# Chunk-selected attention with a gated feed-forward layer: mask halves by block transposes, x scaled on either of two engines, loads planned with a margin, first block's turns leading

## The chip, the cores and the metric

The kernel runs on one core of a Trainium2 chip. A core has a matrix engine (TensorE, PE in the profile; its weight loads are PEld) and three engines for everything else: VectorE (DVE), ScalarE (ACT) and GpSimd (POOL). SyncE (SP) issues transfers. Each engine takes its instructions strictly in program order and waits at an instruction until its inputs are there. The metric is the device time of the whole program in microseconds (us).

## The reference

```python
# q, k, v: (4, 8, 768, 64); chunks of 32 keys, the 6 best chunks for each query
k_min, k_max = k_chunks.min(3), k_chunks.max(3)
ub = sum_d max(q * k_min, q * k_max)              # upper bound of the score of each chunk
ub = where(causal, ub, -1e9); top = argsort(ub)[..., -6:]
scores = where(chunk in top and key <= query, q @ k.T / 8, -1e9)
attn = softmax(scores) @ v                        # -> x: (3072, 512)
xn = x / sqrt(mean(x * x) + 1e-6) * rms_g
g, val = xn @ w_gate, xn @ w_val                  # 512 -> 1536
out = (g * sigmoid(g) * val) @ w_out              # 1536 -> 512
```

## The kernel before

The work is cut into 12 blocks of 256 tokens (4 batches by 3). Each block goes through an attention part (two jobs of four heads) and a feed-forward part (`ffn`). A small planner in the kernel's Python (`Plan`) holds all operations with a guessed length, a priority and their inputs, and simulates the engines: the order that comes out of the simulation is the program. It does not run on the chip. An operation made with `flex` can go to any of several engines; the planner picks one. A lower priority number comes first among what is ready at the same time.

```python
PACE, LEAD = 23.0, 60.0
def due_attn(i): return PACE * i - LEAD      # priority of block i's attention
def due_ffn(i):  return PACE * i             # and of its feed-forward part
SPLIT = {0}                                  # the first block: its two halves of tokens apart
...                                          # (cut) in Rings: when a planned transfer lands
op.done = now + (0.9 if op.dma[2] else 1.2)
...                                          # (cut) in job(i, g): one block, four heads
turn("k"); half("k")                         # VectorE: kT by 32x32 block transposes; then kb in bf16
                                             # (ScalarE or GpSimd)
... # ext: minimum and maximum per chunk (VectorE); dk, bd: placed in BD (GpSimd or VectorE)
turn("q"); half("q")                         # qT, qb
... # upper: bounds (TensorE); ubn, bar, top, mk (VectorE): mk = bound below the sixth best
plan.op("mt", "DVE", ... VE.transpose(out=mtd, in_=mk) ...)     # the mask, transposed in 32x32 blocks

def swap():                                  # the mask's two halves of 64 partitions exchanged
    VE.tensor_copy(at(mto)[0:64, 0:nj], at(mtd)[64:128, 0, 0:nj])
    VE.tensor_copy(at(mto)[64:128, 0:nj], at(mtd)[0:64, 1, 0:nj])
def swap_act(): ...                          # the same two copies as ScalarE activations
flex("swap", {"DVE": (0.46, 0.48, swap), "ACT": (0.65, 0.66, swap_act)}, base + 3,
     reads=[mtd], writes=[mto], ...)
... # vx: v in bf16 with a column of ones (GpSimd or ScalarE)
... # scores: q k (L643) plus the mask as matmuls of mtd and mto (L654); exp (ScalarE) -> pt;
    # tri: the causal triangle of pt (GpSimd); values: pt v (L719); rden, norm -> xnat (VectorE)

def norm(i, toks, base):                     # (cut)
    ... # square (ScalarE), rms -> ri_all (GpSimd)
    plan.op("scale", "DVE", 0.265, 0.35, lambda: VE.tensor_scalar(
        out=at(xs), in0=at(xn), scalar1=ri_all[:, tt:tt + 1], scalar2=None, op0=ALU.mult), ...)
    ... # turn: xs transposed on TensorE (L779); xsT: scaled by rms_g (ScalarE or VectorE)

def ffn(i, toks):                            # (cut)
    ... # gate matmuls with wg and wv (L817), tanh -> th and vcopy -> vs (ScalarE), tg (VectorE),
        # hh (GpSimd, some on VectorE), project with wo (L849), out -> osb, store

loads(0); loads(1)
dma("rmsg", "SP", moe_rms_g ..., -480, ...)  # priority -480
```

While TensorE would stand idle in the first 60 us of the plan, the planner gives it filler matmuls of the identity (`keep_busy`, L903)[...]. The weights are loaded by GpSimd's queue, after the first `dk`. Blocks 2 and 3 wait with their loads for part of the weights. Nearly all other loads and all stores are issued by SyncE.

Of the kernel before, what the change touches and what calls it, by code (L numbers as in the profile page):

```python
# [10 lines left out]
ALU = mybir.AluOpType  # L11
# [9 lines left out]

class Op:
    __slots__ = ("eng", "occ", "lat", "fn", "pri", "deps", "waits", "done",
                 "takes", "uses", "dma", "ready", "mode", "start", "name", "seq", "users", "alts", "after", "inst")

    def __init__(self, name, eng, occ, lat, fn, pri):
        self.name, self.eng, self.occ, self.lat, self.fn, self.pri = name, eng, occ, lat, fn, pri
        self.deps, self.takes, self.uses, self.users, self.after = [], [], [], [], []
        self.dma = None
        self.mode = None  # L30
        self.done = None
        self.alts = {eng: (occ, lat, fn)}


class Rings:
# [34 lines left out]
    def add(self, t, ring, packets, cost, op):  # L70
        self._step(min(t, self.wait[0][0]) if self.wait else t)

        def landed(now, op=op):
            op.done = now + (0.9 if op.dma[2] else 1.2)
        op.done = None
        self.wait.append((t, ring, [packets, cost, landed]))
        self.wait.sort(key=lambda w: w[0])
        self.guess()
# [28 lines left out]
class Plan:  # L107

    SHARES = ("scale", "swap", "relu", "bd0", "bd1", "dk", "mk")
    HOP = {"PE": 0.055, "ACT": 0.04, "DVE": 0.04, "POOL": 0.075, "SP": 0.06}

    def __init__(self):
# [35 lines left out]
    def run(self, in_order=(), fill=None):  # L150
# [55 lines left out]
        while todo:  # L206
            best = None
            for e, c in cand.items():
                if not c:
                    continue  # L210
                rows = [(est(o, e), o) for o in c]
                rows = [(t, o) for t, o in rows if t is not None]
                if not rows:
                    continue
                t0 = max(at[e], min(t for t, o in rows))
                t, o = min(((t, o) for t, o in rows if t <= t0 + 1e-9),
                           key=lambda r: (r[1].pri, r[1].seq))
                if best is None or (t0, o.pri) < (best[0], best[1].pri):
                    best = (t0, o, e)
            if best is None:  # L220
                stuck = [o.name for c in cand.values() for o in c][:12]
                raise RuntimeError(f"no op can go on: {stuck}")
            t, o, e = best
            todo -= 1
            if e == "PE" and fill is not None:
                begin, cold, end, step, pool, fn = fill
                t0 = max(begin, at[e])
                f = [x for x in self.free[pool] if x[0] + 0.055 <= t0]
                t1 = min(t, end) - (0.11 if o.mode != "full" else 0.03)
                n = int(max(0.0, min(t1, cold) - t0) / (2 * step) + max(0.0, t1 - max(t0, cold)) / step)  # L230
                if n > 0 and f:
                    w = Op("warm", "PE", t1 - t0, t1 - t0, lambda n=n, x=f[0][1]: fn(n, x), 0)
                    w.seq, w.start, w.mode = -1, t0, "full"
                    w.done = at[e] = t1
                    mode = "full"
                    order.append(w)
            for x in o.alts:
                cand[x].remove(o)
            o.eng = e
            o.occ, o.lat, o.fn = o.alts[e]  # L240
            if e == "PE" and mode is not None and mode != o.mode:
                t += 0.105
            if e == "PE":
                mode = o.mode
            o.start = t
            if e in port and shares(o, e):
                port[e] = (t, t + o.lat - 0.06)
            at[e] = t + o.occ
            o.done = t + o.lat
            if o.dma is not None:  # L250
                packets, cost, hw = o.dma
                rings.add(t + o.occ + (0.6 if hw else 1.4), e, packets, cost, o)
                if hw:
                    at[e] = max(at[e], rings.room(e, t))
                if hw:
                    lanes.append(o)
            for key in o.takes:
                p = self.pool_of[key]
                if p in strict:
                    head[p] += 1  # L260
                self.free[p].sort()
                slot[key] = self.free[p].pop(0)[1]
            for key in o.uses:
                last[key] = max(last.get(key, 0.0), o.done)
                left[key] -= 1
# [13 lines left out]
def kernel(  # L279
# [41 lines left out]
    def at(key):  # L321
        return store[plan.pool_of[key]][plan.slot[key]]
# [46 lines left out]
    ORDER = [(0, 0), (1, 0), (2, 0), (3, 0), (0, 1), (1, 1), (0, 2), (2, 1), (1, 2),  # L369
             (3, 1), (2, 2), (3, 2)]  # L370
    assert sorted(ORDER) == [(b, m) for b in range(B) for m in range(NBLK)]
    PACE, LEAD = 23.0, 60.0
    SPLIT = {0}
    PACKED = {0, 1, 2}
    DIRECT = {(i, hp) for i in range(len(ORDER)) for hp in range(KH) if i >= 6 and hp % 2}
# [10 lines left out]
    def dma(name, eng, src, dst, packets, cost, pri, writes, takes=(), reads=(), behind=()):  # L386
        occ = {"SP": 0.49 if pri < -400 else 0.57, "ACT": 0.46, "POOL": 0.78}[eng]

        def start():
            o.inst = issuer[eng].dma_start(out=dst(), in_=src)  # L390
            for p in fences:
                tc.add_manual_dep(o.inst.ins, p.inst.ins.name, mybir.DependencyInfo(
                    mybir.DependencyClass.Sync, mybir.DependencyReason.DATA), reason="order")

        fences = [p for key in behind for p in plan.wrote[key]]
        o = plan.op(name, eng, occ, occ, start, pri,
                    reads=list(reads) + list(behind), writes=writes, takes=takes)
        o.dma = (packets, cost, eng != "POOL")
        return o

    def flex(name, alts, pri, **kw):
# [94 lines left out]
    def job(i, g):  # L496
# [2 lines left out]
        w = 64 if m == 0 else BLK  # L499
        nj = w // 64  # L500
        base = due_attn(i) + 0.5 * g
        early = i < 2
        kraw, qraw, vraw = ("kraw", b, m), ("qraw", b, m), ("vraw", b, m)
        kT, qT, kb, qb, kx = ("kT", *J), ("qT", *J), ("kb", *J), ("qb", *J), ("kx", *J)
        bd = ("BD", b, g)
# [1 line left out]
        def turn(nm):  # L507
            raw, T = (nm + "raw", b, m), (nm + "T", *J)
            fast = i not in PACKED
            tokens = "p h (j r) -> p j h r" if fast else "p h (r j) -> p j h r"  # L510
            plan.op(f"turn {nm}{J}", "DVE", 0.6 if fast else 0.94, 0.7 if fast else 1.10,
                    lambda: VE.transpose(out=at(T).rearrange(tokens, r=32, j=8),
                                         in_=at(raw)[:, g]),
                    base + (0 if nm == "k" else 1), reads=[raw],
                    writes=[T], takes=[(T, nm + "T")])

        def half(nm):
            T, hb = (nm + "T", *J), (nm + "b", *J)
            act = lambda: SE.activation(out=at(hb), in_=at(T), func=ACT.Copy)
            pool = lambda: GE.tensor_copy(at(hb), at(T))  # L520
            flex(f"half {nm}{J}", {"ACT": (0.54, 0.63, act), "POOL": (0.57, 0.61, pool)},
                 base + 2, reads=[T], writes=[hb], takes=[(hb, nm + "b")])

        turn("k")
        half("k")
# [84 lines left out]
            base + 3, reads=[mk], writes=[mtd], takes=[(mtd, "mtd")])  # L610

        def swap():
            VE.tensor_copy(at(mto)[0:64, 0:nj], at(mtd)[64:128, 0, 0:nj])
            VE.tensor_copy(at(mto)[64:128, 0:nj], at(mtd)[0:64, 1, 0:nj])

        def swap_act():
            SE.activation(out=at(mto)[0:64, 0:nj], in_=at(mtd)[64:128, 0, 0:nj], func=ACT.Copy)
            SE.activation(out=at(mto)[64:128, 0:nj], in_=at(mtd)[0:64, 1, 0:nj], func=ACT.Copy)

        flex(f"swap{J}", {"DVE": (0.46, 0.48, swap), "ACT": (0.65, 0.66, swap_act)}, base + 3,  # L620
             reads=[mtd], writes=[mto], takes=[(mto, "mto")])
        vx = ("VX", *J)
        vin, vout = (lambda: at(vraw)[:, :, g]), (lambda: at(vx)[:, :, :, 0:D])
        flex(f"vx{J}", {
            "POOL": (0.57, 0.62, lambda: GE.tensor_copy(vout(), vin())),
            "ACT": (0.54, 0.63, lambda: SE.activation(out=vout(), in_=vin(), func=ACT.Copy)),
        }, base + 4, reads=[vraw] + ones, writes=[vx], takes=[(vx, "VX")])


        pts = {}  # L630
# [114 lines left out]
    def norm(i, toks, base):  # L745
# [20 lines left out]
                writes=[("ri", *U)])  # L766
        for s in toks:
            xn, xs, tt = ("xnat", b, m, s), ("xs", i, s), 2 * blk + s
            plan.op(f"scale{i}{s}", "DVE", 0.265, 0.35, lambda xn=xn, xs=xs, tt=tt: VE.tensor_scalar(
                out=at(xs), in0=at(xn), scalar1=ri_all[:, tt:tt + 1], scalar2=None, op0=ALU.mult),  # L770
                base, reads=[xn, ("ri", *U)], writes=[xs], takes=[(xs, "xs")])

        def tview():
# [99 lines left out]
    def loads(i):  # L873
# [3 lines left out]

    loads(0)
    loads(1)
    dma("rmsg", "SP", moe_rms_g.rearrange("(g p) -> p g", p=P), lambda: rmsg[:], 32, 0.018, -480,  # L880
        writes=["rmsg"])
    for i in range(len(ORDER)):
        if i > 1:
            loads(i)
# [52 lines left out]
```

## Time and profile before

| | |
|---|---|
| median time of the program | 320.17 us |
| span of the profiled execution | 320.3 us |
| scaling of xs, VectorE, 128x512 | 24, mean 543 ns |
| square, ScalarE, 128x512 | 24, mean 630 ns |
| mask transpose mtd, VectorE, 128x256 / 128x64 | 16, mean 429 ns / 8, mean 241 ns |
| swap copies on VectorE, 64x128 (the two lines) | 5 of 191 ns and 5 of 554 ns in the mean |
| swap copies on ScalarE, 64x128 / 64x32 | 22 of 307 ns / 14 of 228 ns |
| xsT on ScalarE / on VectorE (whole) | 32 rows of 487 ns / 3 of 1219 ns |
| filler matmuls | 328, 23.1 us busy |

In the page, a busy share is time in which an engine had an instruction running. A busy TensorE need not be doing wanted work: filler counts too, and a matmul at a lower granted clock takes longer. The table by stage gives for each stretch of 10 us the busy time of each engine with the number of its instructions in brackets, then the granted TensorE clock (1.00 is full speed), the share of the 16 DMA engines that were busy, and GB/s. In the timeline each line has its start, its length, engine, line and operation; the brackets tell how long the engine stood idle before and who released it.

### The profile page before, as it was taken

To read this page: it belongs to the slowest core of one execution; us is meant where nothing else is said; L and a number is where in the kernel's file an instruction comes from. 1 tells how busy PE (TensorE), PEld (TensorE's weight loads), DVE (VectorE), ACT (ScalarE), POOL (GpSimd) and SP (SyncE) were. 2 spreads that over 40 slices of the span, in tenths; PEclk is the share of its full clock that TensorE was granted. 3 is DMA by queue.
4 is the path that set the end of the run, shared out by engine and by line. 5 is a ranking of instruction groups with operands and counts; after the bars stand their busy time and mean duration, and the time that the engine had idled before them with its cause. 6 is when DMAs were issued, how large, how long until landed. Compare 5 with 4: busy or idle time off the path is not lost.

```text
span 320.3 us, 11960 instructions
## 1 busy us (share of the span) xinstructions
PE 302.4 (94%) x4952; PEld 235.4 (73%) x4952; DVE 220.5 (69%) x599; ACT 216.2 (68%) x393; POOL 156.4 (49%) x287
## 2 busy tenths in 40 slices
PE   8788999979998999879999999999999999999994
PEld 8687886865865877656788687788587688678681
DVE  6877499895998998968956836496465366437360
ACT  2566746974768896496797686679579469665240
POOL 4774493876764777488656353155133114213120
PEclk9999999998999999979999999999999999999999
DMA  8999986576564647775310300100010110010101
GB/s 183 220 239 207 251 160 150 112 197 142 149 134 118 141 109 174 163 165 114 99 39 19 115 5 2 68 3 4 33 37 0 36 37 2 36 35 2 65 2 65
DMA packets 74838, 30.66 MB, mean 96 GB/s; under 512 B 65568, under 2 KB 70176, under 8 KB 74784
## 3 DMA queue, kind: packets, MB, share of 16 engines
q1 hardware_dynamic: 69712, 24.66, 31.5%
q0 software_dynamic: 4752, 4.72, 8.9%
q8 instruction: 39, 0.64, 0.8%
q10 hardware_dynamic: 320, 0.52, 0.6%
q14 instruction: 15, 0.12, 0.1%
HBM read 28.31 MB, written 6.29 MB: 108 GB/s over the span
## 4 chain that ended last, share of the span: by engine, by line
PE 69%; DVE 8%; DMA 7%; SPq 7%; ACT 4%; issue 3%; POOL 1%; DVEq 0%; ACTq 0%
PE F L817 30%; PE F L849 17%; SPq L390 6%; PE F L719 6%; PE S L643 6%; PE S L574 4%; DMA kraw<-in_k_dram 3%; DMA qraw<-in_q_dram 3%; PE S L654 2%; PE F L903 2%; DMA vraw<-in_v_dram 2%; DVE kx L527 2%; PE F L779 1%; DVE tg L828 1%; ACT pt L693 1%
## 5 line engine op out<-in xcount | busy, mean ns | idle before, releaser
L693 ACT ACTIVATE pt<-S 128x1024 bf16<-128x1024 f32 (+3 forms) x100 | 86.2, 887 | 25.8 <-PE S L654 24.8
L839 POOL TENSOR_TENSOR hh<-tg,vs 128x512 bf16<-128x512 bf16 x54 | 62.3, 1157 | 64.1 <-ACT vs L836 40.7
L828 DVE SCALAR_TENSOR_TENSOR tg<-th,F 128x512 bf16<-128x512 bf16 x72 | 48.8, 681 | 44.1 <-ACT th L824 37.9
L817 PE MATMUL F<-xsT,wg 128*128 128x256 bf16 (+1 forms) x624 | 76.0, 267 | 1.7 <-DVE xnat L738 1.7
L817 PE MATMUL F<-xsT,wv 128*128 128x256 bf16 (+1 forms) x624 | 75.8, 266 | 0.5 <-DVE tg L828 0.5
L849 PE MATMUL F<-wo,hh 128*128 128x512 bf16 x288 | 68.2, 381 | 0.0
L817 PEld LDWEIGHTS <-wg 128*128 128x128 bf16 x624 | 56.4, 99 | 10.8 <-issue 2.7
L817 PEld LDWEIGHTS <-wv 128*128 128x128 bf16 x624 | 55.8, 98 | 8.1 <-issue 1.0
L824 ACT ACTIVATE th<-F 128x512 bf16<-128x512 f32 x72 | 43.0, 602 | 15.0 <-PE F L817 13.5
L663 POOL TENSOR_SCALAR_AFFINE_SELECT pt<-pt 128x512 bf16<-128x512 bf16 x48 | 31.2, 654 | 42.8 <-ACT pt L693 42.4
L849 PEld LDWEIGHTS <-hh 128*128 128x128 bf16 x288 | 26.5, 98 | 27.9 <-issue 0.8
L643 PE MATMUL S<-qb,kb 32*128 32x256 bf16 (+1 forms) x784 | 33.3, 257 | 3.3 <-ACT pt L693 2.0
L836 ACT ACTIVATE vs<-F 128x512 bf16<-128x512 f32 x54 | 32.4, 600 | 4.4 <-PE F L817 3.3
L527 DVE TENSOR_REDUCE kx<-kT 128x16 f32<-128x512 f32 x48 | 30.8, 663 | 0.0
L719 PE MATMUL F<-VX,pt 128*128 128x65 bf16 x672 | 26.9, 195 | 3.7 <-ACT vs L836 3.0
L719 PEld LDWEIGHTS <-pt 128*128 128x128 bf16 x672 | 24.9, 99 | 6.0 <-ACT pt L693 2.3
L865 DVE TENSOR_SCALAR osb<-F 128x512 f32<-128x512 f32 x17 | 11.6, 687 | 24.7 <-PE F L849 24.6
L643 PEld LDWEIGHTS <-kb 32*128 32x128 bf16 x784 | 14.0, 92 | 15.5 <-issue 13.7
L903 PE MATMUL F<-ident 128*128 128x128 bf16 x328 | 23.1, 232 | 2.1 <-POOL ident masks.py:199 1.4
L903 PEld LDWEIGHTS <-ident 128*128 128x128 bf16 x328 | 20.8, 105 | 2.8 <-POOL ident masks.py:199 1.4
L654 PE MATMUL S<-mtd,chunkrow 32*128 32x128 bf16 (+2 forms) x384 | 20.9, 204 | 0.6 <-issue 0.6
L654 PEld LDWEIGHTS <-chunkrow 32*128 32x128 bf16 x768 | 19.3, 94 | 2.4 <-issue 1.4
(60 smaller groups left out, 374.4 us busy)
## 6 DMA issues: line engine op xcount, KB each, us to landing
vraw<-in_v_dram SPq DMA_DIRECT2D x24, 256.0 KB, 4.2
out_dram<-osb SPq DMA_DIRECT2D x24, 256.0 KB, 2.1
kraw<-in_k_dram SPq DMA_DIRECT2D x72, 64.0 KB, 2.8
qraw<-in_q_dram SPq DMA_DIRECT2D x72, 64.0 KB, 2.3
wg<-in_moe_w_gate_dram POOLq DMA_DIRECT2D x3, 512.0 KB, 11.9
wv<-in_moe_w_val_dram POOLq DMA_DIRECT2D x3, 512.0 KB, 11.6
wo<-in_moe_w_out_dram POOLq DMA_DIRECT2D x3, 512.0 KB, 17.5
kraw<-in_k_dram SPq DMA_DIRECT2D x10, 128.0 KB, 5.4
```

Source lines behind the costliest of these rows:

```text
L527: plan.op(f"ext{n}{J}", "DVE", 0.585, 0.67, lambda n=n, op=op: VE.tensor_reduce(out=at(kx)[:, n], in_=at(kT).rearrange("p h (c t) -> p h c ...
L643: TE.matmul(s[a // 2][:, a % 2, c0:c0 + q1 - q0], kbt[r, t, ks], qbt[r, t, q0:q1], start=(t == 0), stop=(t == 1 and not mask), skip_group_ ...
L654: TE.matmul(o, chunkrow[r, BLK * kg + P * e:BLK * kg + P * (e + 1)], mv, start=False, stop=(d == 1), skip_group_check=True)
L693: lambda pt=pt, hs=hs, c0=c0, c1=c1, x=sc[hp]: SE.activation(out=at(pt)[:, hs, c0:c1], in_=at(x)[:, :, c0:c1], func=ACT.Exp, scale=SCALE), ...
L719: TE.matmul(o[:, a, :], p_[:, a, off:off + P], vt[:, e, a, :], start=(kb_ == 0 and a == 0), stop=(kb_ == nkb - 1 and a == 3), skip_group_c ...
L817: TE.matmul(at(p_)[:, n * W:(n + 1) * W], w[:, g, ht * P:(ht + 1) * P], at(xT)[:, g, 0:W], start=(g == 0), stop=(g == NP - 1), skip_group_ ...
L824: plan.op(f"tanh{U}.{hp}", "ACT", 0.48, 0.6, lambda th=th, gp=gp: SE.activation(out=at(th), in_=at(gp), func=ACT.Tanh, scale=0.5), pri, re ...
L828: VE.scalar_tensor_tensor(out=at(tg), in0=at(th), scalar=1.0, in1=at(gp), op0=ALU.add, op1=ALU.mult), pri - 30, reads=[th, gp], writes=[tg ...
L836: plan.op(f"vcopy{U}.{hp}", "ACT", 0.48, 0.6, lambda vs=vs, vp=vp: SE.activation(out=at(vs), in_=at(vp), func=ACT.Copy), pri + 0.1, reads= ...
L839: plan.op(f"hh{U}.{hp}", "POOL", 1.11, 1.16, lambda tg=tg, vs=vs, hh=hh: GE.tensor_tensor(out=at(hh), in0=at(tg), in1=at(vs), op=ALU.mult) ...
L849: TE.matmul(at(op)[:], at(("hh", *U, ht // K))[:, o:o + P], wo[:, ht, :], start=(ht == 0), stop=(ht == NHT - 1))
L903: TE.matmul(store["F"][slot][:, 0:P], ident[:], ident[:], start=True, stop=True)
```

## The change

- **Mask halves.** On VectorE the swapped mask is no longer copied from the transposed mask `mtd`: it is transposed from `mk` once more, with the halves of the partitions exchanged. It needs `mk` and not `mtd`. ScalarE's form is as before.
- **Scale.** x times its reciprocal root mean square can be done by VectorE or ScalarE.
- **Margin.** In the plan, a load issued by SyncE with a priority above -30 (the later ones) counts as landed 3 us later. The attention's lead over the feed-forward part is 70 rather than 60.
- **First block.** Turns, halves and v of the first block have a priority number lower by 8, so they come ahead of the chunk extremes.
- **rmsg** is loaded by ScalarE's queue, after the first q.
- Two small repairs in the planner: filler takes the buffer that has been free longest, and no transfer starts before 2.3 us in the plan. `PATIENT` is empty, so its branch does nothing. Swaps no longer count as using the port that VectorE and GpSimd share, in the plan.

```diff
-            op.done = now + (0.9 if op.dma[2] else 1.2)
+            op.done = now + (0.9 if op.dma[2] else 1.2) + op.slack
...
-    SHARES = ("scale", "swap", "relu", "bd0", "bd1", "dk", "mk")
+    SHARES = ("scale", "relu", "bd0", "bd1", "dk", "mk")
+    PATIENT = {}
...
-                f = [x for x in self.free[pool] if x[0] + 0.055 <= t0]
+                f = sorted(x for x in self.free[pool] if x[0] + 0.055 <= t0)
...
-                rings.add(t + o.occ + (0.6 if hw else 1.4), e, packets, cost, o)
+                rings.add(max(2.3, t + o.occ + (0.6 if hw else 1.4)), e, packets, cost, o)
...
-    PACE, LEAD = 23.0, 60.0
+    PACE, LEAD = 23.0, 70.0
+    MARGIN = 3.0
+    FIRST = 8
...
+        o.slack = MARGIN if pri > -30 and eng == "SP" else 0.0
...
+        first = FIRST if i in SPLIT else 0
...                                  (turn)
-                    base + (0 if nm == "k" else 1), reads=[raw],
+                    base + (0 if nm == "k" else 1) - first, reads=[raw],
...                                  (half)
-                 base + 2, reads=[T], writes=[hb], takes=[(hb, nm + "b")])
+                 base + 2 - first, reads=[T], writes=[hb], takes=[(hb, nm + "b")])
...                                  (swap)
-            VE.tensor_copy(at(mto)[0:64, 0:nj], at(mtd)[64:128, 0, 0:nj])
-            VE.tensor_copy(at(mto)[64:128, 0:nj], at(mtd)[0:64, 1, 0:nj])
+            for r, c, h in ((slice(0, 64), slice(64, 128), 0), (slice(64, 128), slice(0, 64), 1)):
+                VE.transpose(out=at(mto)[r].rearrange("p j c -> p (j c)")[:, 0:32 * nj],
+                             in_=at(mk)[c, h].rearrange("p j c -> p (j c)")[:, 0:32 * nj])
...
-        flex(f"swap{J}", {"DVE": (0.46, 0.48, swap), "ACT": (0.65, 0.66, swap_act)}, base + 3,
-             reads=[mtd], writes=[mto], takes=[(mto, "mto")])
+        flex(f"swap{J}", {"DVE": (0.42 if m else 0.28, 0.5 if m else 0.36, swap), "ACT": (0.65, 0.66, swap_act)}, base + 3,
+             reads=[mtd, mk], writes=[mto], takes=[(mto, "mto")])
...                                  (vx)
-        }, base + 4, reads=[vraw] + ones, writes=[vx], takes=[(vx, "VX")])
+        }, base + 4 - first, reads=[vraw] + ones, writes=[vx], takes=[(vx, "VX")])
...                                  (scale)
-            plan.op(f"scale{i}{s}", "DVE", 0.265, 0.35, lambda xn=xn, xs=xs, tt=tt: VE.tensor_scalar(
-                out=at(xs), in0=at(xn), scalar1=ri_all[:, tt:tt + 1], scalar2=None, op0=ALU.mult),
+            flex(f"scale{i}{s}", {
+                "DVE": (0.265, 0.35, lambda xn=xn, xs=xs, tt=tt: VE.tensor_scalar(
+                    out=at(xs), in0=at(xn), scalar1=ri_all[:, tt:tt + 1], scalar2=None, op0=ALU.mult)),
+                "ACT": (0.54, 0.63, lambda xn=xn, xs=xs, tt=tt: SE.activation(
+                    out=at(xs), in_=at(xn), func=ACT.Copy, scale=ri_all[:, tt:tt + 1]))},
...
-    dma("rmsg", "SP", moe_rms_g.rearrange("(g p) -> p g", p=P), lambda: rmsg[:], 32, 0.018, -480,
+    dma("rmsg", "ACT", moe_rms_g.rearrange("(g p) -> p g", p=P), lambda: rmsg[:], 32, 0.018, -480,
...
+    plan.ops[-1].after.append([o for o in plan.ops if o.dma and o.name.startswith("load q00")][-1])
```

Which engine each operation lands on and where each stands is decided by the planner when the program is built, so a small edit can reorder everything after it.

More of the change, by code (lines that the diff above doesn't have):

```diff
@@ L23 @@
     __slots__ = ("eng", "occ", "lat", "fn", "pri", "deps", "waits", "done",
-                 "takes", "uses", "dma", "ready", "mode", "start", "name", "seq", "users", "alts", "after", "inst")
+                 "takes", "uses", "dma", "ready", "mode", "start", "name", "seq", "users", "alts", "after", "inst", "slack")
     def __init__(self, name, eng, occ, lat, fn, pri):
@@ L29, in __init__ @@
         self.dma = None
+        self.slack = 0.0
         self.mode = None
@@ L215, in run @@
                 t0 = max(at[e], min(t for t, o in rows))
-                t, o = min(((t, o) for t, o in rows if t <= t0 + 1e-9),
-                           key=lambda r: (r[1].pri, r[1].seq))
+                now = sorted(((t, o) for t, o in rows if t <= t0 + 1e-9),
+                             key=lambda r: (r[1].pri, r[1].seq))
+                t, o = now[0]
+                if e in self.PATIENT:
+                    soon = [r for r in rows if r[0] <= t0 + self.PATIENT[e]]
+                    for t, o in now + sorted(soon, key=lambda r: (r[1].pri, r[1].seq)):
+                        end = t + o.alts[e][0] - 0.1
+                        if not any(t < r[0] < end and r[1].pri < o.pri - 10 for r in soon):
+                            break
+                    t0 = max(t0, t)
                 if best is None or (t0, o.pri) < (best[0], best[1].pri):
@@ L501, in job @@
         base = due_attn(i) + 0.5 * g
-        early = i < 2
+        first = FIRST if i in SPLIT else 0
         kraw, qraw, vraw = ("kraw", b, m), ("qraw", b, m), ("vraw", b, m)
```

## The prediction

> **What bounds the kernel now.** I read the page first, then the table by stage, then TensorE's own timeline for its gaps, then the chain of waits. From the page:
>
> ```profile
> PE 302.4 (94%) x4952; PEld 235.4 (73%) x4952; DVE 220.5 (69%) x599; ACT 216.2 (68%) x393; POOL 156.4 (49%) x287
> ...
> DMA  8999986576564647775310300100010110010101
> ```
>
> TensorE is busy nearly throughout, but part of that is filler (matmuls of the identity, line 903, which keep its clock up); DMA is full only in the first 40 us. So the span is a start, then TensorE's work, plus its gaps. The table by stage (time, busy and count for PE, PEld, DVE, ACT, POOL, then granted clock, DMA share, GB/s) says where the gaps are:
>
> ```profile
> 60.00:70.00 10.00, 9.17 (x168) 7.69 (x161) 9.17 (x26) 9.92 (x23) 8.01 (x15) 1.00 0.72 182
> 70.00:80.00 10.00, 8.64 (x80) 4.63 (x79) 6.59 (x18) 4.25 (x9) 6.12 (x10) 0.83 0.59 132
> ...
> 90.00:100.00 10.00, 8.66 (x110) 5.09 (x107) 9.91 (x18) 7.32 (x15) 5.06 (x10) 1.00 0.46 101
> ...
> 130.00:140.00 10.00, 6.33 (x119) 5.25 (x116) 6.99 (x21) 6.36 (x13) 5.94 (x10) 0.97 0.67 145
> 140.00:150.00 10.00, 10.00 (x127) 7.21 (x125) 8.97 (x21) 7.96 (x15) 8.20 (x13) 0.86 0.82 169
> ```
>
> From 150 us to the last projection TensorE has no gap over 0.2 us. The loss is all earlier: 130 to 140 us lacks 3.67, 60 to 100 us lacks 3.5, and twice the clock falls after a gap (0.83, 0.86). The timeline of the stretches that matter (start, length, engine, line, what, and in brackets the idle time before it):
>
> ```profile
> 25.11 0.31 DVE L769 TENSOR_SCALAR xs<-xnat,ri_all 128x512 bf16<-128x512 bf16 x1
> 25.47 0.40 PE L779 MATMUL F<-ident,xs 128*128 128x128 bf16 x4
> 25.91 1.14 ACT L788 ACTIVATE xsT<-F,rmsg 128x128 bf16<-128x128 bf16 x4
> 27.90 1.06 PE L817 MATMUL F<-xsT,wg 128*128 128x128 bf16 x16
> ...
> 41.86 4.85 PE L903 MATMUL F<-ident 128*128 128x128 bf16 x84
> ...
> 71.36 1.87 PE L817 MATMUL F<-xsT,wg 128*128 128x256 bf16 x8 [1.68 <-DVE xnat L738]
> ...
> 134.27 0.63 ACT L626 ACTIVATE VX<-vraw 128x512 bf16<-128x512 f32 x1 [3.31 <-DMA vraw<-in_v_dram]
> ...
> 136.35 0.22 PE L719 MATMUL F<-VX,pt 128*128 128x65 bf16 x2 [1.65 <-ACT vs L836]
> ```
>
> First: the first real matmul of the feed-forward part starts at 27.90; its input xs was ready for scaling at 22.84 (the two ri_all instructions on GpSimd end there), but VectorE runs in program order and first turned block 1's q, which the chain of waits shows landing at 21.5 (13.50 + 8.04). Second: at 41.86 TensorE is given 4.85 us of filler. Third: at 134.27 ScalarE has stood 3.31 us for a v load that was planned to be there; the exponentials behind it, and TensorE behind those, stop (1.65, 0.70 and 1.32 us).
>
> **What the Trainium skill says.** "SBUF — State Buffer", section "Who interferes with whom": a VectorE copy or tensor_scalar in a two-port mode and a GpSimd instruction exclude each other for the whole instruction, and ScalarE waits for neither. The trace agrees: the 24 scalings of xs on VectorE take 306 ns at best, 351 in the median and 1275 at worst; the half-swaps on VectorE (64x128) 190 in the median and 1114 at worst. The block transpose of the mask (128x256, mean 429 ns) shows no such spread. "DMA: Bandwidth & Descriptors", section "Issuing engines are not separate DMA queues": all queues share 16 DMA engines, so moving the small rmsg load to ScalarE's queue saves issue time only. Its issue takes 0.42 us at the head of SyncE's queue, and k's first issue there is at 1.27. "TensorE: Matmul & The Clock Gate", section "What's actually happening": an idle TensorE falls to half clock and must be busy some microseconds to get it back. The trace shows the cost even after the 1.68 us gap: eight gate matmuls in 1.87 us that elsewhere take 1.04.
>
> **The change part by part.** The orders of both programs can be listed from the build, without times; what I count below is from there.
>
> *Start.* rmsg leaves SyncE: k, q and v are issued 0.48 us earlier. With the first block leading, VectorE makes all four turns (kT, kT, qT, qT, about 1.05 us each) before the chunk extremes. From k at 5.5: turns until about 10.2 (q must land by 8), extremes to 12.7, subtract and place to 13.8, both upper bounds on TensorE to 14.8 (before: 12.5 and 14.3, so the second bound is no earlier). Both heads' unmasked scores now go before it, so the first half of the tokens is normalized about 17.0 rather than 20.86, squared by 17.9, its root by 18.9. Then xs of the first half is on ScalarE, behind kb of block 1: VectorE turns block 1's k at about 17 to 19.5, ScalarE's halves end 20.3, xs 20.3 to 20.95 (0.63, as the 128x512 square takes), TensorE's turn 0.4, xsT 1.14: 22.6. No VectorE wait for block 1's q is on that path. But one other is: TensorE has the second head's masked scores ahead of its first gate, and their mto now comes from VectorE behind qT of block 1. If q lands at 20.5 to 21.5, the turn 1.1, mtd 0.24 and two small transposes give mto at 23.3, scores 0.5: first gate at **24.0** against 27.9, **-3.9**. Two upper bounds and eight values matmuls that stood before the gate now follow it: **+1.3** (0.5 each and 0.3).
>
> *Filler.* 328 to 275 matmuls. What stands before the first gate is inside the 24.0. After it, 84 becomes 58 (3, 11, 4, 32, 8): 26 x 0.0565 us (4.69 us for 84 is 56 ns) = **-1.5**. This is real saving only because the order was also changed: xs of block 1 is scaled before VectorE turns block 2's k, where it came 5.7 us later, at 46.85.
>
> *Scale on two engines.* 13 of 24 go to ScalarE: VectorE -13 x 0.543 = -7.1 us, ScalarE +13 x 0.63 = +8.2. In return 20 fewer xsT rows on ScalarE (-20 x 0.487 = -9.7) and 5 more full xsT on VectorE (+5 x 1.219 = +6.1). The rest nearly cancels too: 3 outputs from VectorE to ScalarE (-2.1, +1.8), more of the small bound arithmetic on VectorE (+4 of kx, +5 of BD, relu: about +3.8), 4 more casts and one VX on ScalarE (+3.1), and four small swaps off it (-1.8).
>
> *Swap.* 10 swaps on VectorE, 14 on ScalarE (6 and 18 before). Five are of 128 columns and five of 32. Between the measured 241 ns (64 columns) and 429 (256), a 64x128 transpose is an estimated 0.30 and a 64x32 one 0.20: 10 x 0.30 + 10 x 0.20 = 5.0 against 4.1 for the old copies: +0.9. What it buys is that mto no longer follows mtd and is free of the port. Sum: VectorE about +1.6, ScalarE +1.6, GpSimd -6. None is the bound, so this is worth nothing in itself; it changes which one is late.
>
> *Loads with margin.* No load is faster. The planner lets consumers of later loads count on 3 us more, so the in-order engines put other work ahead of them. The gap of 3.67 and its clock loss (24 gates in 3.72 us at 140.74 instead of 2.7: 1.0) are what it is for. The attention part is also given 10 us more lead.
>
> *Gaps in total.* After the first gate there are now 7.95 us of idle TensorE (0.60, 0.50, 1.68, 0.44, 0.90, 1.65, 0.70, 1.32, 0.16) and about 2.2 of clock (0.83 + 0.37 at 71 to 80 us, 1.0 at 141). I expect most of the load stall to go (-4.7 at the most, I take -3.5), and the others to be exchanged for similar ones: 10.15 becomes about 6.6, **-3.5**.
>
> Sum: -3.9 + 1.3 - 1.5 - 3.5 = -7.6, and 320.2 - 7.6 = **312.5 us**. TensorE's matmul work is the same (139 changes of tile shape in both orders), and the tail too (projection 24, the last gates, projection 24, store, 4.3 us after the last projection).
>
> **Rivals.** *The weights hold the first gate.* Their DMAs wait for the first subtraction, now about 11.4 instead of 9.25, and two mask selects stand between the first and second pair. wg takes 7.8 to 13.3 us to land (11.9 in the median), which from 12.5 is 20 to 26. For: DMA is full until 40 us. Against: then q and k have the DMA to themselves for 2 us more. Worth +2: 314.5. *The DMA-bound start gives the gain back.* Block 2's k waits for the last wv (17.6 us in SyncE's queue), and an earlier feed-forward part could stand at block 2's attention. Against: VectorE did not wait for that data at 41.10. Then only 2 us of lead stay: 315.5. *New stalls.* The plan is fixed at build, the port conflicts are not in it; VectorE is over 90% busy from 40 to 130 us in most stages and an in-order queue that is late once makes TensorE and its clock late. Idle stays at 10 or grows to 13: 316 to 319. *All gaps close.* TensorE runs through from 24 us, with 2 us of gaps: 308.
>
> **Range and chances.** The rivals that cost give 314 to 319, the one that helps 308; I put the range at 306.5 to 318.5. A gain over 2% means below 313.8, hardly above my number, and three of four rivals lie past it: 0.54. Within 2%: 0.42. Slower by 2% (326.6) needs several new stalls at once: 0.04.
>
> **What would show it.** Right: first gate at 23 to 25 us; no ScalarE wait of over 1 us for v near 130; TensorE's gaps after the first gate 4 to 8 us; xs on ScalarE near 0.63 us, the 64x128 transposes 0.25 to 0.35 with little spread; filler 58 after the gate. Wrong: a first gate at 26 or later with a wait for wg; a new gap of over 2 us between 40 and 130 us with the clock below 0.9 after it; VectorE the releaser of TensorE's gaps.

## The result and the profile after

The changed kernel takes **308.87 us** in the median (308.56 to 309.58) against 319.34 before. One of the four executions of the kernel before took 1039.74 us; the ratio, 0.970 with an interval of 0.963 to 0.977, is to the mean of the other three (316.71, 318.51 and 320.17), and by it the gain is 9.5 us. The prediction was 312.5, in a range of 306.5 to 318.5.

The page of the changed kernel, the lines that answer to those of before:

```profile
PE 294.1 (96%) x4876; PEld 229.5 (75%) x4899; DVE 218.1 (71%) x606; ACT 217.7 (71%) x386; POOL 150.9 (49%) x272
...
DMA  8999995785754712754666100100010010110101
```

Busy times of VectorE and ScalarE hardly moved (-2.4 and +1.5, where the prediction's count gave +1.6 for each); of TensorE's 8 us less, 3.6 are filler (23.1 to 19.5 us). The table by stage, the same stretches as before (columns as there: PE, PEld, DVE, ACT, POOL busy, granted clock, DMA share, GB/s):

```profile
60.00:70.00 10.00, 9.43 (x173) 6.12 (x171) 8.04 (x23) 6.93 (x15) 6.06 (x9) 1.00 0.77 190
70.00:80.00 10.00, 9.24 (x167) 7.60 (x152) 8.38 (x30) 8.37 (x16) 6.99 (x12) 1.00 0.72 179
...
90.00:100.00 10.00, 9.95 (x171) 7.28 (x174) 8.83 (x31) 7.21 (x13) 4.28 (x6) 1.00 0.41 110
...
130.00:140.00 10.00, 10.00 (x197) 8.42 (x197) 8.96 (x28) 9.94 (x19) 7.42 (x13) 1.00 0.62 141
140.00:150.00 10.00, 9.89 (x134) 6.39 (x134) 7.96 (x17) 7.29 (x10) 4.80 (x10) 1.00 0.44 108
```

The hole of 3.67 us at 130 to 140 is gone and no stretch shows a clock below 1.00. The timeline of the start, and of the place where the filler of 84 stood (start, length, engine, line, what, idle before):

```profile
18.19 0.72 ACT L786 ACTIVATE xs<-xnat,ri_all 128x512 bf16<-128x512 bf16 x1
...
19.69 1.11 DVE L525 STREAM_TRANSPOSE qT<-qraw 128x512 f32<-128x512 f32 x1 [1.32 <-DMA qraw<-in_q_dram]
...
20.90 0.20 PE L668 MATMUL S<-mtd,chunkrow 32*128 32x32 bf16 x4 [0.46 <-DVE rden L748]
...
21.71 1.07 PE L834 MATMUL F<-xsT,wg 128*128 128x128 bf16 x16
...
39.12 0.72 ACT L786 ACTIVATE xs<-xnat,ri_all 128x512 bf16<-128x512 bf16 x1
39.22 0.35 DVE L784 TENSOR_SCALAR xs<-xnat,ri_all 128x512 bf16<-128x512 bf16 x1
...
40.00 0.61 PE L796 MATMUL F<-ident,xs 128*128 128x128 bf16 x8
...
40.28 1.12 DVE L525 STREAM_TRANSPOSE kT<-kraw 128x512 f32<-128x512 f32 x1 [0.72 <-DMA kraw<-in_k_dram]
```

The first gate comes at 21.71 (27.90 before); the second head's mask is the last thing it waits for, as predicted. Block 1's x is scaled at 39.12 and 39.22, on both engines at once and ahead of block 2's k; TensorE turns it at 40.00 (48.27 before). In the kernel before, the same two operations stood at:

```profile
46.85 0.61 DVE L769 TENSOR_SCALAR xs<-xnat,ri_all 128x512 bf16<-128x512 bf16 x2
...
48.27 0.61 PE L779 MATMUL F<-ident,xs 128*128 128x128 bf16 x8
```

What TensorE waits for after its first gate adds up to 3.95 us in the timeline (7.95 before). Of these, 2.03 us are two gaps at 26.15 and 32.08 (0.88 and 1.15). What ended them stays open: the profile names nothing for the first, and for the second a product hh that had ended 0.48 us before. Gaps of 0.3 to 2.0 us near 26 and 32 us stand in most of the runs below.

Taken as a sum between the two profiled executions: first gate -6.2, named waits -4.0, filler -0.8, the rest of TensorE's time -2.5 (it holds the matmuls moved behind the gate; if the prediction's estimate of +1.3 for them is right, clock and closeness of issue gave -3.8): -13.5, which is 306.8 - 320.3. That is 4 us more than the gain of 9.5: the profiled execution of the kernel before took 321.97 us, with its clock down twice. A sum of this kind only says where time left. Which part of the change took it, and whether the parts add, is for the experiments.

### The profile page after: what moved, and what is told of

Read it like the earlier page. It is cut to its first block, busy times and chain, and to the rows that moved or that the text cites. A ratio compares the mean times of both kernels' runs of the same rounds, so it can differ in the third digit from the quotient of the medians.

```text
span 306.8 us, 11811 instructions
## 1 busy us (share of the span) xinstructions
PE 294.1 (96%) x4876; PEld 229.5 (75%) x4899; DVE 218.1 (71%) x606; ACT 217.7 (71%) x386; POOL 150.9 (49%) x272
## 4 chain that ended last, share of the span: by engine, by line
PE 84%; DMA 3%; ACT 3%; SPq 3%; issue 2%; POOL 2%; DVE 2%; ACTq 0%; DVEq 0%; POOLq 0%
PE F L834 40%; PE F L866 20%; PE S L657 7%; PE F L733 7%; PE S L587 6%; PE S L668 3%; SPq L402 3%; DMA qraw<-in_q_dram 2%; PE F L796 2%; DMA kraw<-in_k_dram 1%; ACT th L841 1%; POOL hh L856 1%; PE F L921 1%; POOL pt L677 1%; ACT pt L707 1%
## 5 line engine op out<-in xcount | busy, mean ns | idle before, releaser
L834 PE MATMUL F<-xsT,wg 128*128 128x256 bf16 (+1 forms) x624 | 74.9, 265 | 0.2 <-DVE xnat L752 0.2
L834 PE MATMUL F<-xsT,wv 128*128 128x256 bf16 (+1 forms) x624 | 74.9, 264 | 0.0
L866 PE MATMUL F<-wo,hh 128*128 128x512 bf16 x265 | 64.7, 379 | 1.4 <-issue 0.5
L657 PE MATMUL S<-qb,kb 32*128 32x256 bf16 (+1 forms) x784 | 32.5, 255 | 1.4 <-ACT qb L532 1.1
L540 DVE TENSOR_REDUCE kx<-kT 128x16 f32<-128x512 f32 x48 | 29.8, 663 | 0.0
L733 PEld LDWEIGHTS <-pt 128*128 128x128 bf16 x672 | 24.0, 98 | 3.6 <-POOL hh L856 1.3
L882 DVE TENSOR_SCALAR osb<-F 128x512 f32<-128x512 f32 x14 | 9.4, 686 | 19.5 <-PE F L866 19.4
L768 ACT ACTIVATE junk<-xnat 128x512 bf16<-128x512 bf16 x24 | 15.1, 629 | 10.6 <-DVE xnat L752 10.1
L921 PE MATMUL F<-ident 128*128 128x128 bf16 x275 | 19.5, 232 | 1.4 <-POOL ident masks.py:199 1.4
L668 PE MATMUL S<-mtd,chunkrow 32*128 32x128 bf16 (+2 forms) x384 | 20.3, 203 | 0.5 <-DVE rden L748 0.5
L668 PE MATMUL S<-mto,chunkrow 32*128 32x128 bf16 (+2 forms) x384 | 20.2, 203 | 0.2
```

Of the source, the lines that this page charges most:

```text
L540: plan.op(f"ext{n}{J}", "DVE", 0.585, 0.67, lambda n=n, op=op: VE.tensor_reduce(out=at(kx)[:, n], in_=at(kT).rearrange("p h (c t) -> p h c ...
L657: TE.matmul(s[a // 2][:, a % 2, c0:c0 + q1 - q0], kbt[r, t, ks], qbt[r, t, q0:q1], start=(t == 0), stop=(t == 1 and not mask), skip_group_ ...
L668: TE.matmul(o, chunkrow[r, BLK * kg + P * e:BLK * kg + P * (e + 1)], mv, start=False, stop=(d == 1), skip_group_check=True)
L733: TE.matmul(o[:, a, :], p_[:, a, off:off + P], vt[:, e, a, :], start=(kb_ == 0 and a == 0), stop=(kb_ == nkb - 1 and a == 3), skip_group_c ...
L834: TE.matmul(at(p_)[:, n * W:(n + 1) * W], w[:, g, ht * P:(ht + 1) * P], at(xT)[:, g, 0:W], start=(g == 0), stop=(g == NP - 1), skip_group_ ...
L866: TE.matmul(at(op)[:], at(("hh", *U, ht // K))[:, o:o + P], wo[:, ht, :], start=(ht == 0), stop=(ht == NHT - 1))
```

## The experiments

All are times of the whole program, median of 4 executions or more. "First gate" and "waits" (of TensorE after it, summed from its timeline) are from each run's profile; "filler" counts the filler matmuls after the first gate in the program.

| run | us | first gate | waits | filler |
|---|---|---|---|---|
| before | 319.34 | 27.90 | 7.95 | 84 |
| after | 308.87 | 21.71 | 3.95 | 58 |
| e1 60 filler more at the start | 311.93 | 24.59 | 4.55 | 58 |
| e2 no filler after the gate | 308.39 | 22.05 | 3.45 | 0 |
| e3 FIRST = 0 | 311.41 | 23.45 | 2.96 | 99 |
| e4 MARGIN = 0 | 311.49 | 21.40 | 5.36 | 59 |
| e5 scale on VectorE only | 314.30 | 20.69 | 8.08 | 57 |
| e6 old swap, planned anew | 310.68 | 21.35 | 4.30 | 65 |
| e7 old swap in the same order | 308.86 | 21.47 | 3.59 | 58 |
| e8 before + start | 316.94 | 19.96 | 8.71 | 127 |
| e9 before + start + scale | 313.95 | 21.18 | 7.39 | 65 |
| e10 LEAD = 60 | 310.65 | 21.95 | 4.85 | 62 |
| e11 MARGIN = 3.5 | 309.59 | 22.50 | 2.51 | 58 |
| e12 LEAD = 72, MARGIN = 2 | 308.17 | 21.06 | 3.57 | 59 |

The kernel before, run again beside them, had medians of 317.7 to 318.4; the ratios given below are to those. Its time goes with its granted clock: nine executions at 0.999 or more took 315.5 to 316.7 us, seven at 0.983 or 0.984 took 319.7 to 320.8. Against the first nine the change is worth about 7.6 us (316.32 and 308.67 in the median at such a clock), so some 2 of the 9.5 us are clock.

The changed kernel was not run again beside the experiments, so differences to its 308.87 also hold what moved between rounds of runs (0.7 us in the medians of the kernel before). No run has rmsg's move or the two repairs of the planner alone.

**e1: does a lead at the first gate reach the end?** The changed order, with 60 filler matmuls more just ahead of the last wait before the gate.

```diff
...
-        o.fn()
+    gate = [o.name.startswith("wg(") for o in todo].index(True)
+    last = [o for o in todo[:gate] if o.name == "warm"][-1]
+    for o in todo:
+        if o is last:
+            o.fn(o.fn.__defaults__[0] + 60)
+        else:
+            o.fn()
```

> The changed kernel, its order kept, with 60 more filler matmuls put before the first gate matmul (60 x 0.0565 = 3.4 us, of which some 0.7 us of waiting for the second head's mask absorbs, so the first gate moves from 21.7 to about 24.4). Theory 'start': TensorE's order sets the end from the first gate on, so the end moves by the same 2.7 us, 308.9 to 311.6. Rival 'slack later' (later waits for data set the pace, an early lead is lost at them): the end moves by less than 1 us, and the TensorE gaps after the first gate shrink from about 3.5 us to under 2.

Its timeline has the added filler, and the gate behind it:

```profile
20.71 3.52 PE L921 MATMUL F<-ident 128*128 128x128 bf16 x60 [0.33 <-issue]
...
24.59 1.07 PE L834 MATMUL F<-xsT,wg 128*128 128x128 bf16 x16
```

The gate moved by 2.88 us, the time by 3.06 (311.64 to 312.74 against 308.56 to 309.58; ratio to the kernel before 0.981, 0.975 to 0.988). In the changed order the first gate counts one to one; the waits after it did not shrink to take the delay up.

**e2: is filler a cost?** The same order, the 58 filler matmuls after the gate left out.

```diff
-        o.fn()
+        gated = gated or o.name.startswith("wg(")
+        if o.name != "warm" or not gated:
+            o.fn()
```

> The changed kernel, its order kept, without the 58 filler matmuls after the first gate (58 x 0.0565 = 3.3 us). Theory 'filler stands where TensorE would wait anyway': the time stays within 1 us of 308.9, gaps take the place of the filler, and if the clock falls after them it gets slower. Rival 'filler is cost' (as the term of 1.5 us in the prediction takes it): up to 3.3 us faster, 305.6.

308.39, 0.5 us less for 3.3 us of filler taken away; the ranges overlap (308.30 to 309.38). Where 32 filler matmuls stood, there is now the first of these lines, and block 2's scaling is waited for longer than in the changed kernel (0.91 against 0.47):

```profile
40.21 1.80 PE L834 MATMUL F<-xsT,wg 128*128 128x256 bf16 x8 [0.56 <-ACT xsT L805]
...
63.40 0.62 PE L796 MATMUL F<-ident,xs 128*128 128x128 bf16 x8 [0.91 <-DVE xs L784]
```

The changed kernel has these gates 2.0 us later, and faster:

```profile
42.23 1.04 PE L834 MATMUL F<-xsT,wg 128*128 128x256 bf16 x8
```

Without the filler they run in step with ScalarE's four pieces of xsT (weight loads at 40.22, 40.58, 40.95 and 41.31), so 0.76 us of the lead goes there, 0.40 in a wait for block 2's qT at 45.19, and by 63.40 it is 0.26 us. The granted clock was 1.00 from 39 to 43 us, without filler. Filler mostly covers waits: all 58 together cost 0.5 us. So fewer filler matmuls are a sign that something came earlier, and not a saving to be added up at 56 ns each.

**e3: the first block's priorities.**

```diff
-    FIRST = 8
+    FIRST = 0
```

> The changed kernel with FIRST = 0, all else kept. Theory 'start': the first gate comes about 2 us later than 21.7, and the time is 2 us longer, 311. Rival 'margin and order later': the first gate still moves, but the time stays within 1 us of 308.9 because what matters are the stalls after 60 us.

311.41 (+2.5; ratio 0.979, 0.973 to 0.985), gate at 23.45 (+1.7), near what "start" expected, and filler 99: in this order block 1's scaling stands behind block 2's k again (46.28 and 46.69), and TensorE's turn of it at 47.83. Its waits after the gate are fewer than in the changed kernel (2.96), so a part of the loss is made good there. The gate is still 4.45 us earlier than in the kernel before: with rmsg moved and the first half's xs on ScalarE (20.21, as soon as its root is there at 20.18), most of the gate's gain comes without FIRST, too.

**e4: the margin.**

```diff
-    MARGIN = 3.0
+    MARGIN = 0.0
```

> The changed kernel with MARGIN = 0. Theory 'margin': stalls for late loads of v or k come back, TensorE idles 2 to 4 us near 100 to 140 us and its clock falls after it: 312 to 314. Rival 'start': the margin is worth little, within 1 us of 308.9.

311.49 (+2.6; ratio 0.980, 0.973 to 0.987), just below the 312 to 314 that "margin" expected. The view of waits (who waited for what: us in total, times, longest) for all waits on transfers, first of e4, then of the changed kernel:

```profile
POOL VX L639 <- DMA vraw<-in_v_dram: 3.0, 3, 1.1
POOL pt L677 <- DMA kraw<-in_k_dram: 2.7, 1, 2.7
ACT VX L640 <- DMA vraw<-in_v_dram: 2.4, 1, 2.4
DVE kT L525 <- DMA kraw<-in_k_dram: 2.4, 2, 2.2
DVE qT L525 <- DMA qraw<-in_q_dram: 1.8, 3, 0.7
```

```profile
DVE qT L525 <- DMA qraw<-in_q_dram: 1.9, 2, 1.3
POOL hh L856 <- DMA qraw<-in_q_dram: 1.3, 1, 1.3
DVE kT L525 <- DMA kraw<-in_k_dram: 1.1, 2, 0.7
ACT VX L640 <- DMA vraw<-in_v_dram: 0.4, 1, 0.4
```

Waits of ScalarE and GpSimd for v (5.4 us, as against 0.4) come back without the margin, and with them the wait of 2.4 us on ScalarE at 135 us. Little of it reaches TensorE, though: about 2 us of waits between 128 and 140 us, none as long as the 1.65 of before. The profiled execution also had a gap of 1.96 us at 26.92, where the changed kernel has 0.88, and a granted clock of 0.90 from 20 to 30 us; it was the longest of the four. Nor does the hole at 130 to 140 us need the margin to close. e10, with the margin and the old lead, has no TensorE wait there; and neither has e9, which has neither margin nor the longer lead:

```profile
130.00:140.00 10.00, 10.00 (x149) 7.56 (x138) 9.70 (x24) 9.72 (x17) 8.98 (x14) 1.00 0.96 186
```

A new order is enough. That the margin is what closed it is not shown.

**e5: scaling of x on VectorE only.**

```diff
-            flex(f"scale{i}{s}", {"DVE": (0.265, 0.35, ...), "ACT": (0.54, 0.63, ...)},
+            plan.op(f"scale{i}{s}", "DVE", 0.265, 0.35, ...,
```

> The changed kernel with the scaling of x on VectorE only. The prediction's reason (xs on ScalarE is what frees the first gate from VectorE's queue): the first gate moves back from 21.7 to 23 or later and the time is 2 us or more longer, 311. Rival (the first block's priorities do it, the scaling engine does not matter): the first gate stays within 0.7 us of 21.7, and the time changes only by what later stalls do, within 1.5 us.

314.30 (+5.4; ratio 0.988, 0.983 to 0.994), the most that any single part is worth, yet the first gate came *earlier* (20.69). So ScalarE's scaling is not what frees the gate. The view of tile xs in e5 has what it costs: first the scalings (min, median, max in ns), then who waited for them (us, times):

```profile
L783 DVE TENSOR_SCALAR xs<-xnat,ri_all x24: 312/534/1268, 17.9 to 279.1; 128x512 bf16<-128x512 bf16 x24
...
  ACT xsT L802: 7.9, 7
  PEld L793: 3.4, 6
  PE F L793: 2.0, 4
```

The same view of the changed kernel:

```profile
L786 ACT ACTIVATE xs<-xnat,ri_all x13: 710/722/754, 18.2 to 277.5; 128x512 bf16<-128x512 bf16 x13
L784 DVE TENSOR_SCALAR xs<-xnat,ri_all x11: 346/349/1240, 28.8 to 277.3; 128x512 bf16<-128x512 bf16 x11
...
  ACT xsT L805: 1.6, 3
  PEld L796: 0.8, 2
  PE F L796: 0.5, 1
```

Two scalings of a block in a row on VectorE can make TensorE's turn late: at 40 us e5 takes 1.53 us for the pair while GpSimd's product hh runs (started 40.17), and the second half of the turn waits 0.58. Four turns of e5 wait in this way, 1.97 us in all. On two engines the halves go side by side, and ScalarE's form, though twice as long as VectorE's best, never varies by more than 44 ns. TensorE's waits are 8.08 us against 3.95, but the waits for xs are only 1.5 us of this difference; the longest other one is 1.40 us at 93.75. The rest of the 5.4 us can be the new order, and no run changes the scaling's engine with the order held.

**e6 and e7: the swap.** e6 puts the old copies back in plan and program; e7 keeps the plan and the order of the changed kernel and only emits the old copies in the ten places.

```diff
-                VE.transpose(out=at(mto)[r]..., in_=at(mk)[c, h]...)     # both
+            VE.tensor_copy(at(mto)[0:64, 0:nj], at(mtd)[64:128, 0, 0:nj])
+            VE.tensor_copy(at(mto)[64:128, 0:nj], at(mtd)[0:64, 1, 0:nj])
-        flex("swap", {"DVE": (0.42 if m else 0.28, ...), ...}, reads=[mtd, mk], ...)   # e6 only
+        flex("swap", {"DVE": (0.46, 0.48, swap), ...}, reads=[mtd], ...)
```

> The changed kernel with the old swap in plan and program (two copies of mtd on VectorE or ScalarE). Theory 'swap is worth nothing in itself': within 1 us of 308.9. Rival 'swap off the shared port removes stalls': 1 to 4 us longer, with copies of about 1 us on VectorE ahead of a TensorE gap.

> The changed kernel, plan and order kept, but the ten VectorE swaps are emitted as the old copies of mtd. The one thing that differs is the instruction. Theory 'swap is worth nothing in itself': within 0.5 us of 308.9, though some copies take 0.5 to 1.1 us rather than 0.19. Rival 'port': 1 us or more longer.

e7 takes 308.86, the same to 0.01 us. The view of tile mto in e7 (min/median/max, ns) and then in the changed kernel:

```profile
L626 DVE COPY mto<-mtd x10: 170/258/1140, 20.1 to 234.4; 64x32 bf16<-64x32 bf16 x5, 64x128 bf16<-64x128 bf16 x5
L627 DVE COPY mto<-mtd x10: 168/188/677, 20.9 to 234.6; 64x32 bf16<-64x32 bf16 x5, 64x128 bf16<-64x128 bf16 x5
```

```profile
L627 DVE STREAM_TRANSPOSE mto<-mk x20: 205/256/307, 20.9 to 234.6; 64x32 bf16<-64x32 bf16 x10, 64x128 bf16<-64x128 bf16 x10
```

The transposes do what they are for: never over 307 ns, where copies reach 1140. It buys nothing here: TensorE's waits are 3.59 us with the copies and 3.95 with the transposes. e6 is 1.8 us slower (ratio 0.977, 0.971 to 0.982). With e7 beside it that is not the instruction: the other planned lengths, inputs and port rule gave another order. The size is what the rival expected of e6; its reason is refuted by e7.

**e8: the start alone**, put into the kernel before (first block's turns, halves and v leading; rmsg on ScalarE's queue).

> The kernel before with the start's part alone: turns, halves and v of the first block leading, rmsg on ScalarE's queue. Theory 'start': the first gate comes at about 22 rather than 27.9 us, and a good part of the whole gain is there: 313 to 315. Rival 'margin and order later': the first gate comes earlier but the stalls for v near 130 us stay and the time is within 2 us of the kernel before.

316.94 (20 executions; ratio 0.996, 0.993 to 0.998). The first gate comes at 19.96, 7.9 us earlier and the earliest of all, and the program gains 1.4 us. Even these need not be the lead: at a granted clock of 0.999 or more, e8 takes 316.7 us in the median (13 of 20 executions) and the kernel before 316.3. Its timeline shows where the lead went:

```profile
38.56 0.70 POOL L762 TENSOR_TENSOR ri_all<-ri_all,mhalf 128x2 f32<-128x2 f32 x1
...
39.61 5.19 PE L904 MATMUL F<-ident 128*128 128x128 bf16 x90
...
40.68 2.06 DVE L512 STREAM_TRANSPOSE kT<-kraw 128x512 f32<-128x512 f32 x2 [3.38 <-DMA kraw<-in_k_dram]
...
47.34 0.82 DVE L769 TENSOR_SCALAR xs<-xnat,ri_all 128x512 bf16<-128x512 bf16 x2
...
47.96 0.66 PE L779 MATMUL F<-ident,xs 128*128 128x128 bf16 x8 [1.43 <-DVE xs L769]
```

Block 1's x could be scaled at 39.26, where its root ends. But VectorE stands at block 2's k, 3.38 us idle, until the transfer lands, and then does the turns and extremes of block 2 first. TensorE fills 5.19 us, waits 1.43, and at 47.96 is 0.3 us ahead of the kernel before (48.27). Block 2's k lands at about 40.3 in the changed kernel, too: the transfer did not move.

**e9: start and scale together in the kernel before.**

> The kernel before with two parts: the start (first block's turns leading, rmsg on ScalarE's queue) and the scaling of x on either engine. The order has block 1's two scalings ahead of block 2's turns, one of them on ScalarE. Theory 'the lead was lost behind block 2's k' (start alone had its first gate at 19.96 and lost the lead at 47.96, where TensorE waited for block 1's scaled x): block 1's turn comes at about 40 instead of 48 us, the filler after the first gate falls to below 70, and the time is 4 us or more below start alone's 316.9, so 313 or less. Rival 'the transfers bound the start anyway' : block 1's turn is early but a wait for block 2 takes its place before 60 us, and the time stays above 315.

313.95 (ratio 0.990, 0.987 to 0.993), 3.0 us below e8, and between what the two expected: the lead is kept, but not 4 us of it. Its timeline at the same place:

```profile
39.93 0.72 ACT L772 ACTIVATE xs<-xnat,ri_all 128x512 bf16<-128x512 bf16 x1
...
40.03 0.35 DVE L770 TENSOR_SCALAR xs<-xnat,ri_all 128x512 bf16<-128x512 bf16 x1
...
40.65 2.06 DVE L512 STREAM_TRANSPOSE kT<-kraw 128x512 f32<-128x512 f32 x2 [0.27 <-DMA kraw<-in_k_dram]
...
40.71 0.62 PE L782 MATMUL F<-ident,xs 128*128 128x128 bf16 x8
```

The turn comes at 40.71 rather than 47.96 and filler falls from 127 to 65. What it gives back are waits elsewhere, of 0.88, 0.59 and 0.56 us after 267 us; the one of 1.52 us at 72.83 for xnat is an old one (1.68 in the kernel before). e9 changes the engine and the order at once. e5 has block 1's scaling early as well (39.95), with VectorE alone, so its place in the order is what keeps the lead here, and the second engine is one way by which the planner comes to it.

**e10, e11, e12: the plan's two numbers.**

```diff
-    PACE, LEAD = 23.0, 70.0          # e10: 60.0    e12: 72.0
-    MARGIN = 3.0                     # e11: 3.5     e12: 2.0
```

> The changed kernel with LEAD = 60. Theory 'the attention's lead matters': TensorE waits for attention work (xnat, xs, pt) at 60 to 110 us by 2 us more than with 70, time 311 to 312. Rival 'the lead is only one more shuffle of the order': within 1 us of 308.9.

> The changed kernel with MARGIN = 3.5 instead of 3.0, which alters no cost and barely what the plan is meant to do. Theory 'order luck is small': within 0.7 us of 308.9. Rival 'any edit reshuffles the order and moves the time by as much as the parts do': 1.5 us or more away from it, either way.

> The changed kernel with LEAD = 72 and MARGIN = 2.0, chosen among settings of the two as the one whose planned order leaves TensorE fewest gaps after 60 us. Theory 'what is left after the first gate is the plan's own gaps': TensorE's waits between 60 and 120 us (now 1.4 us) vanish and the time is 306.5 to 308. Rival 'margin of 3 is needed on the chip': waits for loads or for VectorE come back and it is 309 or more.

e10: 310.65 (+1.8), between the 1 us of the rival and the 311 to 312 of the theory, with a wait of 1.45 us for xs at 112.36 and three at 58 to 75. e11: 309.59 (+0.7, at the edge of what "order luck is small" allows), for an edit that barely alters what the plan is meant to do. e12: 308.17 (308.09 to 308.27), 0.7 us below the changed kernel and the fastest of all, but not within the 306.5 to 308 expected; between 60 and 120 us TensorE waits 0.76 us there rather than 1.60 (with the 0.16 at 113.50). That is no more than e11's shuffle, in the other direction.

## Why the prediction was right, and where it was not

**Start: right in direction, mis-sized, and one reason wrong.** The step "first gate at 24.0" measured 21.71, earlier than the 23 to 25 that was to show it. The terms that were off: k landed so that the turns began at 4.96 (not 5.5), the upper bounds ran from 12.33 (not 13.8), xs stood at 18.19 (not 20.3; it took 0.72, not 0.63), and block 1's q could be turned at 19.69 (not 20.5 to 21.5). The order of events was the predicted one, down to the second head's mask as the last wait. But "xs of the first half is on ScalarE" as what frees the gate fell: with VectorE alone (e5) and with the start alone (e8) the gate is earlier still. Where the first block's priorities and rmsg's move are in, they are enough without ScalarE (e8); the priorities alone are 1.7 us of the 6.2 in the changed kernel (e3). k's issue on SyncE came 0.47 us earlier, as predicted, but its turns 1.09 (6.05 to 4.96); why the transfer gained as well is not shown.

**What the gate is worth: taken for granted.** The prediction carried -3.9 through to the end. In the changed order that holds one to one (e1). It does not hold by itself: in e8 7.9 us of lead end as 1.4, and at equal clock as nothing. This is the second rival, "the DMA-bound start gives the gain back", nearly as described, and it was dismissed on a wrong reading: that VectorE did not wait for k at 41.10 in the kernel before only says that it came late to it.

**Filler: the count right, the saving mis-read.** After the gate there are 58, as predicted. -1.5 was booked for 26 filler matmuls fewer; the filler after the gate became 0.8 us shorter in busy time (4.85 to 4.07), and leaving out all 58 changes 0.5 us (e2). What was right is the remark beside it, that block 1's scaling now comes before block 2's turns. That is the hinge of the change: e8 and e9 show the lead lost behind it and kept in front of it.

**Scale: "worth nothing in itself" failed.** The engine totals did cancel (VectorE -2.4, ScalarE +1.5), and e5 still costs 5.4 us. Totals were the wrong view; e9 also lies 3.0 us below e8. What the traces show of it is the pair of scalings before each turn, on two engines and one of them out of GpSimd's way: 0.47 us of TensorE waits for xs where e5 has 1.97. How much of the 5.4 is this and how much is another order can't be told apart by e5: edits of no such worth moved 0.7 and 1.8 us (e11, e6).

**Swap: right.** Estimated 0.30 and 0.20, measured 0.306 and 0.206; free of the spread; worth nothing (e7).

**Margin and gaps: the stall went, the reason is not shown, the size was too small.** The load stall is gone. Leaving the margin out costs 2.6 us (e4; predicted 3.5 for this stall), but hardly through this stall, which comes back in e4 only as 1.2 us of short waits at 130 to 140 us, and does not in e9; so part or all of the 2.6 can be order. Waits and clock together were to fall from 10.15 to 6.6 and fell to 3.95: waits by 4.0, just below the 4 to 8 expected, and the clock's part (2.2) went altogether. Of the 1.92 us of waits after 60 us, VectorE ends 1.15; the prediction had named VectorE as the releaser for a sign of being wrong. The clock does not follow from the gap alone: the same gap stands in e8, and the eight gates after it take 1.03, not 1.87.

```profile
71.10 1.03 PE L817 MATMUL F<-xsT,wg 128*128 128x256 bf16 x8 [1.68 <-DVE xnat L738]
```

**The other rivals.** The weights did not hold the first gate: TensorE's only named wait for wg in these traces is 0.16 us in e8, whose gate was the earliest. New stalls of over 2 us did not come. "All gaps close" was nearest in time (308) and wrong in kind: 3.95 us of waits are left.

**The sum.** -7.6 was predicted (from 320.2 this is 312.6, not 312.5), -9.5 measured. The gate's 2.3 us more and the 2.7 more of waits and clock are larger than the difference of 1.9, since they are read from an execution of the kernel before that took 321.97. That 308.87 lies in the range owes much to its width of 12 us; three terms of the sum were off. The parts do not add up to the whole: taken out one at a time, FIRST, margin, scale and lead are worth 2.5 + 2.6 + 5.4 + 1.8 = 12.3, and put into the kernel before, the start alone is worth 1.4.

## What to carry to other kernels

A lead gained at one place can be lost in an in-order queue that stands behind a transfer, as 7.9 us became 0.3 in e8: look for the first instruction on any engine that would wait for data which the change does not speed up, and what stands behind it. When two engines can each do one of a pair of operations that a third engine waits for, look at the time of the pair as well as at the engines' totals. And where a planner lays out the order, test a part by changing the instruction with the order held; leaving the part out and planning anew measures the part and the new order together.

## What had not been expected of the hardware

- A scaled copy on ScalarE with one scale for each partition takes 722 ns for 128x512 bf16, with 710 to 754 as its whole range; the square of the same shape takes 630 and the cast of f32 630 to 634.
- The block transpose between halves of the partitions costs as its columns do, not as its partitions: 64x128 takes 306 ns and 64x32 206, close to the line through 128x64 (225) and 128x256 (427), which gives 292 and 191.
- A TensorE gap of 1.68 us was followed by a slow clock in the kernel before and not in e8, at the same place in the order (eight gate matmuls in 1.87 and 1.03 us, at a granted clock of 0.50 and 1.00). In e8 a gap of 1.32 us at 136.32 was followed by 0.50.
